# Two small weight transfers made twice as wide, and kept in the first ring slot

## The chip, the cores and the metric

The kernel runs on one core of one Trainium2 chip. The metric is the device time of one execution in microseconds; lower is better. Profiles show one execution on the chip. TensorE is PE in them (its weight loads are PEld), VectorE is DVE, ScalarE is ACT, GpSimd is POOL and SyncE is SP, which issues all transfers here.

## The reference

A block for decoding: a layer norm, attention of one new token against a cache, and an MLP, with a residual after each. Batch 4, model width 448, 16 query heads over 8 groups of cached keys and values, head width 256, and the last 1024 positions of the cache.

```python
W = min(4096, max(256, Sk // 4))                    # 1024
q = (x @ wq).reshape(B, Sq, Hq, Dh)...              # [4, 16, 1, 256]
k, v = the last W rows of k_cache and v_cache, each shared by two heads
p = softmax(einsum("bhqd,bhkd->bhqk", q, k) * Dh ** -0.5)
A(x) = einsum("bhqk,bhkd->bhqd", p, v).reshape(B, Sq, Hq * Dh) @ wo
B(x) = gelu(layernorm(x) @ w1 + b1) @ w2 + b2
h = x + A(layernorm(x))
out = h + B(layernorm(h))
```

All is float32. The keys, values and weights that must be read are 88 MB.

## The kernel before, in words

The work goes group by group over the eight groups of keys and values. For a group, `project_q` multiplies the normed input by the group's 448 x 512 query weights and turns the result; `scores` multiplies the query by the keys in two halves of 512 positions; `softmax` and `transpose_p` follow; `values` multiplies by the values; `finish` turns the output and adds its product with the output weights to `acc`. After the last group come the second layer norm and the MLP, with `w1` and `w2`.

The width of 448 is three blocks of 128 rows and one of 64. In the packed weights of a group the last 64 rows lie as 128 rows of 256 columns: the upper half of the partitions holds the second 256 columns. `wq_parts` lists the matmuls of a projection: three with 128 rows and 512 columns, and then either two with 128 rows and 256 columns (each with an input `yT` that is zero in the half that doesn't belong), or, if `last` is given, one with 64 rows and 512 columns.

All data come through a ring of three slots of 128 partitions x 15872 elements (`ring`, filled by `load` at L58), in one queue of transfers on SP, in the order written. The slot `t0` takes the first query weights with the input (`wq0`), and the keys of group 0 with three blocks of the query weights of group 1 (`k0`). The other slots are refilled in turn: `ta` from `la`, `tb` from `lb`, `tc` from `lc`, `td` from `ld`, twice over, and then three slots `te` for the last keys and values and the MLP's weights. The tc load takes the place of `t0`, td that of ta, and so on. Each load waits on SP until the old content of its slot has been read.

The last 64 rows of the query weights of group 1 do not go with `k0`. They come in two transfers of 32 rows of 2048 bytes (L265) into a tile of their own, `wq1_last`; each takes its source from 8 rows of 5 pieces in HBM, of which 4 are read and the fifth is padding. They stand in the queue between `k0` and the first `la`.

The instructions of PE, SP and ACT stand in the order of the code; each engine works through its own, and waits on semaphores.

Of the kernel before, what the change touches and what calls it, by code (L numbers as in the profile page):

```python
# [8 lines left out]
F32 = mybir.dt.float32  # L9
# [6 lines left out]
B, D = 4, 448  # L16
HQ, HKV, SK, DH = 16, 8, 4096, 256
# [3 lines left out]
P = 128  # L21
H = P // 2
# [4 lines left out]
Q = 32  # L27
CACHE = NKC * B * DH
HALF = CACHE // 2
WEIGHTS = 4 * D  # L30
SLOT = CACHE + 2 * WEIGHTS + HALF
COLUMNS = ND * B + 4 + 4 * 4
EPS = 1e-5
SCALE = DH ** -0.5

@with_exitstack
def block_kernel(ctx: ExitStack, tc, wq0, k0, wq1, la, lb, lc, ld, k7, vo, w1, w2, out):
    nc = tc.nc
    const = ctx.enter_context(tc.tile_pool(name="const", bufs=1))
    ring = ctx.enter_context(tc.tile_pool(name="ring", bufs=3))  # L40
    work = ctx.enter_context(tc.tile_pool(name="work", bufs=2))
# [9 lines left out]
    def slot(name):  # L51
        return ring.tile([P, SLOT], F32, tag="r", name=name)

    def load(t, at, src, pieces=None):
        dst = t[:, at : at + src.shape[-1]]
        at = 0
        for n in pieces or (src.shape[-1],):
            nc.sync.dma_start(dst[:, at : at + n], src[:, at : at + n])  # L58
            at += n
        return dst  # L60

    def cut(t, sizes):
        parts, at = [], 0
        for n in sizes:
            parts.append(t[:, at : at + n])
            at += n
        return parts


    def wq_parts(t, last=None):  # L70
        parts = [(a, yT[:, a, :], slice(0, 512), t[:, a * 512 : (a + 1) * 512]) for a in range(3)]
        if last is not None:
            return parts + [(3, yT[:H, 3, :], slice(0, 512), last)]
        for i in range(2):
            parts.append((3, yT[:, 3 + i, :], slice(i * 2 * P, (i + 1) * 2 * P), t[:, 3 * 512 :]))
        return parts


    def keys(t):
        return t.rearrange("p (c b k) -> p c b k", c=2, b=B)  # L80

    def chunks(t):
        v = t.rearrange("p (c b d) -> p c b d", b=B, d=DH)
        return [v[:, c : c + 2] for c in range(0, v.shape[1], 2)]
# [17 lines left out]

    yT = const.tile([P, ND + 1, Q], F32, name="yT")
    nc.vector.memset(yT, 0.0)
    wq1_last = const.tile([H, 512], F32, name="wq1_last")
    zT = const.tile([P, ND, Q], F32, name="zT")
    nc.vector.memset(zT, 0.0)

# [34 lines left out]
    def rsqrt(dst, var, name):  # L143
        ve = work.tile(list(dst.shape), F32, tag="ve", name=f"ve_{name}")
        nc.vector.tensor_scalar_add(ve, var, EPS)
        nc.gpsimd.tensor_tensor(dst, ve, mhalf[: dst.shape[0], : dst.shape[1]], op=ALU.pow)


    def project_q(g, parts):
        pq = ps_m.tile([P, 512], F32, tag="m", name=f"pq{g}")  # L150
        for j, y, cols, w in parts:
            nc.tensor.matmul(pq[j * Q : (j + 1) * Q, cols], y, w, start=True, stop=True)  # L152
        qs = work.tile([P, 512], F32, tag="qs", name=f"qs{g}")
        nc.scalar.copy(qs, pq)  # L154

        pt = ps_m.tile([P, 2 * REP, P], F32, tag="m", name=f"pqt{g}")
        for i in range(2 * REP):
            nc.tensor.transpose(pt[:, i, :], qs[:, i * P : (i + 1) * P], ident)  # L158
        sm = work.tile([P, 2 * REP, B], F32, tag="sm", name=f"sm{g}")
        nc.vector.tensor_reduce(  # L160
            sm, pt.rearrange("p i (j q) -> p i q j", j=4)[:, :, :B, :], axis=AX.X, op=ALU.add
        )

        src = sm.rearrange("p (r c) b -> p c b r", r=REP)
        for i in range(2):
            nc.vector.tensor_copy(qT[g % 2][:, :, :, i * REP : (i + 1) * REP], src)
# [13 lines left out]
    def softmax(g, parts):  # L180
        halves, mx = zip(*parts)
        nm = work.tile([P, 1], F32, tag="nm", name=f"nm{g}")
        nc.vector.tensor_max(nm, mx[0], mx[1])
        nc.vector.tensor_scalar_mul(nm, nm, -SCALE)  # L184
        p = once.tile([P, 2 * 512], F32, tag="p", name=f"p{g}")
        sums = work.tile([P, 2], F32, tag="sums", name=f"sums{g}")
        for h in range(2):
            nc.scalar.activation(  # L188
                p[:, h * 512 : (h + 1) * 512], halves[h], AF.Exp, bias=nm, scale=SCALE,
                accum_out=sums[:, h : h + 1],  # L190
            )
        rec = work.tile([P, 1], F32, tag=f"rec{g % 3}", name=f"rec{g}")
        nc.vector.tensor_add(rec, sums[:, 0:1], sums[:, 1:2])
        nc.vector.reciprocal(rec, rec)
        return p, rec

    def scores(g, kt):
        return [scores_half(g, h, kt[h]) for h in range(2)]

    def transpose_p(g, p):  # L200
        for h in range(2):
            pt = ps_t.tile([P, 4, P], F32, tag="t", name=f"ppt{g}_{h}")
            for c in range(4):
                nc.tensor.transpose(pt[:, c, :], p[:, (4 * h + c) * P : (4 * h + c + 1) * P], ident)  # L204

            src = pt.rearrange("p (c i) (b q) -> p c i b q", i=2, b=B)
            for i in range(2):
                nc.vector.tensor_copy(  # L208
                    pT[g % 2][:, 2 * h : 2 * h + 2, :, i * REP : (i + 1) * REP], src[:, :, i, :, :REP]
                )  # L210


    def values(g, vt, po, pairs=range(NKC // 2)):
        for c in pairs:
            for b in range(B):
                nc.tensor.matmul(  # L216
                    po[b * Q : (b + 1) * Q], pT[g % 2][:, c, b, :], vt[c][:, :, b, :],
                    start=(c == 0), stop=(c == NKC // 2 - 1),
                )
# [35 lines left out]
    def po_tile(g, pool=ps_o, tag="o"):  # L255
        return pool.tile([P, 2, DH], F32, tag=tag, name=f"po{g}")


    t = slot("t0")
    wqt, xT, b2T, b1T = cut(load(t, 0, wq0), (WEIGHTS, ND * B, 4, 4 * 4))  # L260
    wqt = wq_parts(wqt)
    xT = xT.rearrange("p (a b) -> p a b", a=ND)
    ka, kb, wqt1 = cut(load(t, WEIGHTS + COLUMNS, k0), (HALF, HALF, 3 * 512))
    for i in range(2):
        nc.sync.dma_start(  # L265
            wq1_last[i * Q : (i + 1) * Q, :], wq1[i].rearrange("e (p c) -> e p c", c=512)[:, :4, :]
        )
    d = work.tile([P, ND, B], F32, tag="d", name="d_x")
    centred(d, xT, "x")
# [21 lines left out]
        nc.scalar.copy(rs[:, at : at + cols], pr.rearrange("p i c -> p (i c)")[:, :cols])  # L291

    parts = scores(0, [keys(ka), keys(kb)])
    project_q(1, wq_parts(wqt1, wq1_last))
    p, rec = softmax(0, parts)
    transpose_p(0, p)

    def finish(g, po, rec, wt):
        transposed_output(g, po, rec)
        add_output(g, output_weights(wt))  # L300

    for g in (0, 3):
        ka, kb, wqt, va = cut(load(slot(f"ta{g}"), 0, la[g // 3]), (HALF, HALF, WEIGHTS, HALF))
        parts = scores(g + 1, [keys(ka), keys(kb)])
        project_q(g + 2, wq_parts(wqt))
        p, rec_next = softmax(g + 1, parts)
        transpose_p(g + 1, p)
        po = po_tile(g)
        va = chunks(va)
        values(g, va, po, range(0, 2))  # L310

        vb, wot, ka, kb = cut(load(slot(f"tb{g}"), 0, lb[g // 3]), (HALF, WEIGHTS, HALF, HALF))
        values(g, va + chunks(vb), po, range(2, 4))
        p, rec_then = softmax(g + 2, scores(g + 2, [keys(ka), keys(kb)]))
# [29 lines left out]
    p, rec_last = softmax(g + 1, scores(g + 1, kt))  # L344
# [212 lines left out]
```

## Time and profile before

| | |
|---|---|
| time, median of 3 runs | 213.93 us (213.82 to 213.99) |
| profiled execution: time | 214.16 us |
| its span, first to last instruction | 212.4 us |
| granted TensorE clock, mean | 0.854 |
| PE busy | 133.9 us (63%) |
| DVE busy | 39.0 us (18%) |
| ACT busy | 22.1 us (10%) |
| data moved | 88.43 MB, mean 416 GB/s |
| packets of the load queue | 3248, 88.30 MB, 96.9% of 16 DMA engines' span |

The span is counted from the first to the last instruction of the core; the time has some 1.8 us more around it. A load is one transfer that is cut into packets, here one per row of the destination, which 16 DMA engines move side by side. It has landed when its last packet has. In a row such as `206.00 1.71 PE L469 ... [0.69 <-DMA te<-w]` the first number is the start, the second the length, and the bracket says how long the engine was idle before and for what.

### The profile page before, as it was taken

The numbers are of one execution on the slowest core, as the hardware profiler recorded it, in microseconds if no ns is written. First come the engines' busy times: TensorE is split into PE (matmuls) and PEld (weight loads), VectorE is DVE, ScalarE is ACT, GpSimd is POOL, SyncE is SP. The second block draws the span as 40 slices with busy tenths as digits, with TensorE's granted clock in tenths as the row PEclk, the third lists the DMA queues.
The fourth block names the chain that finished last, engine by engine and source line by source line (L and its number), as shares of the span: only waits on it lengthen the run. The fifth ranks groups of instructions, "written<-read, shape, count | busy, mean of one in ns | idle before, by whom it ended". The sixth has DMA issues, their size and how long they took to land.

```text
span 212.4 us, 2302 instructions
## 1 busy us (share of the span) xinstructions
PE 133.9 (63%) x976; PEld 48.3 (23%) x976; DVE 39.0 (18%) x170; ACT 22.1 (10%) x54; POOL 5.0 (2%) x16
## 2 busy tenths in 40 slices
PE   0469805843950696288398098138708879978984
PEld 0342201310220221022123023013202323224432
DVE  1520300410230003022013013100301223112310
ACT  2011300300020100030003002001000302010311
POOL 5100000000000000000000000000000000000200
PEclk9999995995896559589969759856985999999999
DMA  7999898999999999999999999999989999999991
GB/s 294 425 396 534 361 488 361 491 394 475 407 395 529 395 407 430 451 403 459 424 424 488 403 395 505 395 430 419 478 350 460 430 429 394 440 400 444 419 384 52
DMA packets 3257, 88.43 MB, mean 416 GB/s; under 512 B 368, under 2 KB 624, under 8 KB 1328
## 3 DMA queue, kind: packets, MB, share of 16 engines
q1 hardware_dynamic: 3248, 88.30, 96.9%
q8 instruction: 7, 0.11, 0.2%
q14 instruction: 2, 0.02, 0.0%
HBM read 88.23 MB, written 0.07 MB: 416 GB/s over the span
## 4 chain that ended last, share of the span: by engine, by line
DMA 78%; PE 16%; SPq 2%; DVE 1%; issue 1%; ACT 1%; ACTq 0%
DMA tb<-lb 22%; DMA ta<-la 21%; DMA td<-ld 20%; DMA te<-w 14%; PE s L172 6%; PE po L216 4%; SPq L58 2%; PE ppt L204 1%; PE pq L152 1%; PE acc L245 1%; PE pa L469 1%; PE py L479 1%; SPq L265 1%; PE pqt L158 1%; ACT qs L154 1%
## 5 line engine op out<-in xcount | busy, mean ns | idle before, releaser
L177 DVE TENSOR_REDUCE mx<-s 128x1 f32<-128x512 f32 x16 | 11.1, 691 | 57.8 <-PE s L172 57.8
L172 PE MATMUL s<-ta,qT 128*32 128x512 f32 x64 | 10.7, 831 | 10.3 <-DMA ta<-la 10.3
L154 ACT COPY qs<-pq 128x512 f32<-128x512 f32 x8 | 4.7, 585 | 113.3 <-PE pq L152 113.3
L188 ACT ACTIVATE p<-s,nm 128x512 f32<-128x512 f32 x16 | 10.9, 687 | 46.1 <-DVE nm L184 46.1
L233 DVE TENSOR_SCALAR o<-po,rec 128x512 f32<-128x512 f32 x8 | 6.0, 750 | 48.5 <-PE po L216 48.5
L216 PE MATMUL po<-tb,pT 128*32 128x512 f32 x32 | 7.2, 1051 | 12.2 <-DMA tb<-lb 12.2
L172 PE MATMUL s<-td,qT 128*32 128x512 f32 x32 | 7.1, 1042 | 12.1 <-DMA td<-ld 12.1
L152 PE MATMUL pq<-tc,yT 128*32 128x512 f32 (+1 forms) x20 | 3.9, 891 | 16.6 <-DMA tc<-lc 16.6
L204 PE MATMUL ppt<-ident,p 128*128 128x128 f32 x64 | 10.5, 287 | 0.7 <-ACT p L188 0.4
L216 PE MATMUL po<-tc,pT 128*32 128x512 f32 x64 | 10.4, 813 | 0.0
L158 PE MATMUL pqt<-ident,qs 128*128 128x128 f32 x32 | 6.6, 341 | 6.0 <-ACT qs L154 6.0
L204 PEld LDWEIGHTS ppt<-ident,p 128*128 128x128 f32 x64 | 6.7, 141 | 6.3 <-ACT p L188 6.3
L160 DVE TENSOR_REDUCE sm<-pqt 128x16 f32<-128x64 f32 x8 | 1.8, 224 | 34.4 <-PE pqt L158 34.4
L216 PE MATMUL po<-te,pT 128*32 128x512 f32 x64 | 7.5, 595 | 0.5 <-DMA te<-vo 0.5
L172 PE MATMUL s<-tb,qT 128*32 128x512 f32 x64 | 7.4, 607 | 0.0
L216 PE MATMUL po<-td,pT 128*32 128x512 f32 x64 | 7.3, 595 | 0.0
L237 PE MATMUL pot<-ident,o 128*128 128x128 f32 x32 | 5.2, 286 | 2.7 <-DVE o L233 2.7
L158 PEld LDWEIGHTS pqt<-ident,qs 128*128 128x128 f32 x32 | 4.2, 169 | 11.4 <-ACT qs L154 9.7
L351 PE MATMUL warm<-idle 128*32 128x512 bf16 x22 | 6.8, 382 | 0.0
L172 PEld LDWEIGHTS s<-ta,qT 128*32 128x32 f32 x64 | 2.6, 148 | 17.7 <-issue 13.7
L208 DVE COPY pT<-ppt 128x16 f32<-128x16 f32 x32 | 4.7, 171 | 7.6 <-PE ppt L204 7.6
L172 PE MATMUL s<-t,qT 128*32 128x512 f32 x32 | 5.4, 833 | 0.5 <-DMA t<-k 0.5
(134 smaller groups left out, 112.4 us busy)
## 6 DMA issues: line engine op xcount, KB each, us to landing
tc<-lc SPq DMA_DIRECT2D x2, 7936.0 KB, 47.0
td<-ld SPq DMA_DIRECT2D x2, 7936.0 KB, 44.0
ta<-la SPq DMA_DIRECT2D x2, 7040.0 KB, 38.1
tb<-lb SPq DMA_DIRECT2D x2, 7040.0 KB, 43.2
te<-vo SPq DMA_DIRECT2D x1, 4992.0 KB, 28.1
t<-k SPq DMA_DIRECT2D x1, 4864.0 KB, 15.8
te<-k SPq DMA_DIRECT2D x1, 4096.0 KB, 37.8
te<-vo SPq DMA_DIRECT2D x1, 3072.0 KB, 14.8
```

Of the source, the lines that this page charges most:

```text
L152: nc.tensor.matmul(pq[j * Q : (j + 1) * Q, cols], y, w, start=True, stop=True)
L154: nc.scalar.copy(qs, pq)
L158: nc.tensor.transpose(pt[:, i, :], qs[:, i * P : (i + 1) * P], ident)
L172: nc.tensor.matmul(s[b * Q : (b + 1) * Q, :], qT[g % 2][:, c, b, :], kt[:, c, b, :], start=(c == 0), stop=(c == 1),)
L177: nc.vector.reduce_max(m, s, axis=AX.X)
L188: nc.scalar.activation(p[:, h * 512 : (h + 1) * 512], halves[h], AF.Exp, bias=nm, scale=SCALE, accum_out=sums[:, h : h + 1],)
L204: nc.tensor.transpose(pt[:, c, :], p[:, (4 * h + c) * P : (4 * h + c + 1) * P], ident)
L208: nc.vector.tensor_copy(pT[g % 2][:, 2 * h : 2 * h + 2, :, i * REP : (i + 1) * REP], src[:, :, i, :, :REP])
L216: nc.tensor.matmul(po[b * Q : (b + 1) * Q], pT[g % 2][:, c, b, :], vt[c][:, :, b, :], start=(c == 0), stop=(c == NKC // 2 - 1),)
L233: nc.vector.tensor_scalar_mul(o, po, rec)
L237: nc.tensor.transpose(pt[:, i, c], o[:, i, c * P : (c + 1) * P], ident)
L351: nc.tensor.matmul(warm[:Q], idle[:, :Q], idle, start=True, stop=True)
```

## The change

The last 64 rows of the query weights of group 2 go the same way as those of group 1. Both stand side by side in `wq_rest`, 64 rows of 1024 columns, which come in the same two transfers, now of 32 rows of 4096 bytes. They are no longer put into a tile of their own but into the slot `t0`, behind the keys of group 0 (`REST`). The first `la` load (`la0`) loses these rows: its query weights are 1536 columns wide instead of 1792. The second (`la1`) stays as it was. The projection of group 2 takes its last block from `rest`, with one matmul instead of two.

```diff
+REST = WEIGHTS + COLUMNS + CACHE + 3 * 512
...
-    wq1_last = const.tile([H, 512], F32, name="wq1_last")
...
     ka, kb, wqt1 = cut(load(t, WEIGHTS + COLUMNS, k0), (HALF, HALF, 3 * 512))
+    rest = t[:H, REST : REST + 2 * 512]
     for i in range(2):
         nc.sync.dma_start(
-            wq1_last[i * Q : (i + 1) * Q, :], wq1[i].rearrange("e (p c) -> e p c", c=512)[:, :4, :]
+            rest[i * Q : (i + 1) * Q], wq_rest[i].rearrange("e (p c) -> e p c", c=2 * 512)[:, :4, :]
         )
...
-    project_q(1, wq_parts(wqt1, wq1_last))
+    project_q(1, wq_parts(wqt1, rest[:, :512]))
...
     for g in (0, 3):
-        ka, kb, wqt, va = cut(load(slot(f"ta{g}"), 0, la[g // 3]), (HALF, HALF, WEIGHTS, HALF))
+        n = WEIGHTS if g else 3 * 512
+        ka, kb, wqt, va = cut(load(slot(f"ta{g}"), 0, la[g // 3]), (HALF, HALF, n, HALF))
         parts = scores(g + 1, [keys(ka), keys(kb)])
-        project_q(g + 2, wq_parts(wqt))
+        project_q(g + 2, wq_parts(wqt, None if g else rest[:, 512:]))
...
-    la = np.concatenate([k[1:5:3], wq[2:6:3], va[0:4:3]], axis=2)
+    la0 = np.concatenate([k[1], wq[2][:, : 3 * 512], va[0]], axis=1)
+    la1 = np.concatenate([k[4], wq[5], va[3]], axis=1)
...
-    wq1 = np.asarray(A_wq).reshape(D, HKV, 512)[3 * P :, 1].reshape(2, 8, 4 * 512)
-    wq1 = np.concatenate([wq1, np.zeros((2, 8, 512), np.float32)], axis=2)
+    wq_rest = np.asarray(A_wq).reshape(D, HKV, 512)[3 * P :, 1:3].reshape(2, 8, 8 * 512)
+    wq_rest = np.concatenate([wq_rest, np.zeros((2, 8, 1024), np.float32)], axis=2)
```

On SP, at the start of the queue, the loads stand as follows before (destination, source, partitions x elements; DMAHW0 to DMAHW7 are the semaphores that transfers raise, PE and DVE those of the engines):

```order
L58 DMA t_129<-wq 128x1828
L58 DMA t_129<-k 128x9728
L265 DMA wq_last<-wq 32x1x512 x2
L58 DMA ta_247<-la 128x14080
L58 DMA tb_321<-lb 128x14080
L58 DMA tc_390<-lc 128x15872 [waits DMAHW0_49,DMAHW1_49,DVE_49,PE_49]
L58 DMA td_450<-ld 128x15872 [waits DMAHW4_49,PE_49]
```

And now:

```order
L60 DMA t_128<-wq 128x1828
L60 DMA t_128<-k 128x9728
L267 DMA t_128<-wq_rest 32x1x1024 x2
L60 DMA ta_246<-la 128x13824
L60 DMA tb_319<-lb 128x14080
L60 DMA tc_388<-lc 128x15872 [waits DMAHW1_49,DMAHW2_49,DMAHW0_49,DMAHW3_49,DVE_49,PE_49]
L60 DMA td_448<-ld 128x15872 [waits DMAHW4_49,PE_49]
```

The order is the same. The two small transfers write into the slot of `wq0` and `k0`, with rows of 1024 elements instead of 512; the la rows have 256 elements less; and the tc load, which takes that slot, waits for the two small transfers as well.

On PE, from the scores of group 1 to the end of the projection of group 2, before:

```order
L172 MATMUL s_0_249<-ta_247,qT_112 32x512 [waits DVE_49,DMAHW4_49,PE_49,Pool_49]
L172 MATMUL s_0_249<-ta_247,qT_112 32x512 x7
L172 MATMUL s_1_260<-ta_247,qT_112 32x512 [waits PE_49]
L172 MATMUL s_1_260<-ta_247,qT_112 32x512 x7
L152 MATMUL pq_271<-ta_247,yT 32x512 [waits PE_49]
L152 MATMUL pq_271<-ta_247,yT 32x512 x2
L152 MATMUL pq_271<-ta_247,yT 32x256 x2
```

And now:

```order
L173 MATMUL s_0_248<-ta_246,qT_111 32x512 [waits DVE_49,DMAHW4_49,PE_49,Pool_49]
L173 MATMUL s_0_248<-ta_246,qT_111 32x512 x7
L173 MATMUL s_1_259<-ta_246,qT_111 32x512 [waits PE_49]
L173 MATMUL s_1_259<-ta_246,qT_111 32x512 x7
L153 MATMUL pq_270<-ta_246,yT 32x512 [waits PE_49]
L153 MATMUL pq_270<-ta_246,yT 32x512 x2
L153 MATMUL pq_270<-t_128,yT 32x512
```

The last two matmuls became one, which reads the first slot; since it comes after the scores of the la load, `t0` is read until then.

More of the change, by code (lines that the diff above doesn't have):

```diff
@@ L36, in block_kernel @@
 @with_exitstack
-def block_kernel(ctx: ExitStack, tc, wq0, k0, wq1, la, lb, lc, ld, k7, vo, w1, w2, out):
+def block_kernel(ctx: ExitStack, tc, wq0, k0, wq_rest, la0, la1, lb, lc, ld, k7, vo, w1, w2, out):
     nc = tc.nc
+    la = (la0, la1)
     const = ctx.enter_context(tc.tile_pool(name="const", bufs=1))
@@ L541 @@
     arrays = {
-        "wq0": np.concatenate([wq[0], xT, b2, b1], axis=1), "k0": k0, "wq1": wq1, "la": la, "lb": lb, "lc": lc, "ld": ld, "k7": k[7], "vo": vo, "w1": w1, "w2": w2,
+        "wq0": np.concatenate([wq[0], xT, b2, b1], axis=1), "k0": k0, "wq_rest": wq_rest, "la0": la0, "la1": la1, "lb": lb, "lc": lc, "ld": ld, "k7": k[7], "vo": vo, "w1": w1, "w2": w2,
     }
```

## The prediction, on record before the changed kernel ran

> **What bounds the kernel now.** I read the page first (its DMA row, the queues, the chain that ended last), then the timeline of the last microseconds, then the stages of the tail, and last the packet records behind the DMA row.
>
> ```profile
> span 212.4 us, 2302 instructions
> ...
> DMA  7999898999999999999999999999989999999991
> ...
> q1 hardware_dynamic: 3248, 88.30, 96.9%
> q8 instruction: 7, 0.11, 0.2%
> q14 instruction: 2, 0.02, 0.0%
> ...
> DMA 78%; PE 16%; SPq 2%; DVE 1%; issue 1%; ACT 1%; ACTq 0%
> ```
>
> The loads keep 16 DMA engines busy for 96.9% of the span; between the first slice and the last the digit is 8 or 9 everywhere. So the time is the bytes that the busiest DMA engine must move, plus a tail. A second thing stands in the queue rows: seven fetches of 16 KB and two of 8 KB of instructions share those engines.
>
> Who waits at the end is in the timeline (start, length, then in brackets the idle time before the piece and its releaser):
>
> ```profile
> 205.34 0.33 ACT L462 COPY gT<-put 64x8 f32<-64x8 f32 x2 [1.19 <-DVE gT L459]
> 206.00 1.71 PE L469 MATMUL pa<-te,gT 128*32 128x448 f32 x16 [0.69 <-DMA te<-w]
> 207.56 0.56 PEld L479 LDWEIGHTS py<-te,gT 128*32 128x32 f32 x24 [0.67 <-DMA te<-w]
> 209.20 0.11 PEld L479 LDWEIGHTS py<-te,gT 128*4 128x4 f32 x8 [0.23 <-DMA te<-w]
> 209.67 0.29 DVE L485 TENSOR_TENSOR res<-py,hb 128x128 f32<-128x128 f32 x1 [4.42 <-PE py L479]
> ```
>
> PE waits for w2 three times, and for its very last piece (`w2t[13]`) at 209.20. The compute chain has its operand gT at 205.34 + 0.33 = 205.67, so it is 0.33 us ahead of the 206.00 at which the data lets PE start. DMA decides the end, but by 0.33 us only.
>
> A load is landed when the slowest of its engines is done. The stages of the tail show that they are not done together (the last two columns are the busy share of the 16 engines and GB/s):
>
> ```profile
> 206.50:207.00 0.50, 0.50 (x12) 0.14 (x6) 0.00 (x0) 0.00 (x0) 0.00 (x0) 1.00 0.89 351
> 207.00:207.50 0.50, 0.50 (x8) 0.00 (x0) 0.00 (x0) 0.00 (x0) 0.00 (x0) 1.00 0.55 215
> 207.50:208.00 0.50, 0.50 (x22) 0.44 (x21) 0.00 (x0) 0.17 (x1) 0.00 (x0) 1.00 0.47 179
> 208.00:208.50 0.50, 0.50 (x20) 0.21 (x15) 0.00 (x0) 0.36 (x1) 0.00 (x0) 1.00 0.11 39
> 208.50:209.00 0.50, 0.50 (x24) 0.39 (x24) 0.00 (x0) 0.00 (x0) 0.00 (x0) 1.00 0.02 7
> ```
>
> From 207 on the share falls 0.55, 0.47, 0.11, 0.02: half of the engines are idle while one works on to the end. Which half is the question of this case.
>
> **Which engines carry the small transfers.** The trace does not name the DMA engine of a packet, but each engine's packets follow one another within some 30 ns, so that 16 chains can be followed from the packet records. This table is worked out from them (end of an engine's part of a load, us; "low" are the eight chains that hold 2048-byte packets):
>
> ```
> first la load, low  : 33.26 33.35 33.38 33.41 33.44 33.51 33.52 33.52
> first la load, high : 32.61 32.70 33.08 33.14 33.15 33.15 33.25 33.27
> first w2 load, all  : 202.80 203.41 203.48 203.56 203.64 203.71 203.75 204.26
>                       204.37 204.52 204.71 204.75 204.79 204.79 204.90 205.36
> first packet 1.72; second load (lb): first chain done 49.24, another 49.73
> third load (lc): first chain done 67.99, that other 69.91; small transfers landed 17.35
> increments of the semaphores of the two 32-row transfers: 9 and 9; of every other load: 16
> 16 KB fetches begin at 38.92 63.78 99.82 127.52 164.07 185.87 202.65; 8 KB fetches at 45.80 201.97
> median packet: 2048 B 84 ns, 3584 B 140, 5376 B 206, 56320 B 2080, 63488 B 2345
> ```
>
> The two small transfers run on eight engines only, four rows each. [...]
>
> A 16 KB fetch holds one engine up by about 1.45 us: the chain that ended at 49.73 in the second load ends at 69.91 in the third, 20.18 later, where the first chain takes 18.75. Of the first six fetches five fell on chains of the high half, and one on a chain that cannot be told from a low one at the same offset; both 8 KB fetches fell on low ones (0.7 to 0.9 us each). The seventh, at 202.65, fell on a chain that would have ended its part of the first w2 load at 203.73. The undisturbed chains up there are the low ones (203.56 to 203.75); the high ones that were never held up stand at 202.80 to 203.48. So the engine that ends last, at 205.36, is a low one: 203.73 + 1.63.
>
> **The change, part by part.**
>
> *Bytes.* 128 KB leave the first la load, whose rows shrink from 56320 to 55296 bytes on all 16 engines, and come back as 2048 more bytes in each of the 64 small rows, on the eight low engines. The time of a 4096-byte packet is not in the trace: between 140 (3584) and 206 (5376) it is 140 + 66 x 512/1792 = 159 ns. Bounds are two 2048-byte packets, 168 ns, and the rate of the large ones, 4096 x 2080/56320 = 151 ns; I take 159. Low engines gain 8 x (159 - 84) = 0.60 us (0.54 to 0.67). The 1024 bytes off a large row are worth 1024 x (2345 - 2080)/7168 = 37.9 ns, over 8 rows 0.30 us for every engine. Sum: low engines end 0.30 us later (0.24 to 0.37), high ones 0.30 us earlier. Bytes in all, and transfers in number, stay.
>
> *Where that ends up.* The last engine is low, so all w2 pieces land 0.30 us later, PE starts at 206.30 instead of 206.00, and the waits at 207.56 and 209.20 move with it: +0.30 us.
>
> *One matmul less in the projection of group 2.* The two 256-column matmuls with 128 rows become one with 64 rows and 512 columns.
>
> ```profile
> L152 PE MATMUL pq<-ta,yT 128*32 128x512 f32 x12 | 2.1, 592 | 0.0
> L152 PE MATMUL pq<-ta,yT 128*32 128x256 f32 x8 | 2.1, 379 | 0.0
> ...
> 34.13 5.40 PE L172 MATMUL s<-ta,qT 128*32 128x512 f32 x32 [7.12 <-DMA ta<-la]
> 39.34 1.05 PE L152 MATMUL pq<-ta,yT 128*32 128x512 f32 x10
> 43.10 1.92 PE L216 MATMUL po<-ta,pT 128*32 128x512 f32 x16
> ...
> PE po L216 <- DMA tb<-lb: 12.2, 2, 6.4
> ```
>
> Each fp32 matmul has two records, so ten become eight: about 2 x 379 - 592 = 0.17 us of overlapped records saved at most. PE then waits up to 6.4 us for tb, so this is worth nothing; tb is what is late next. The cover would have to shrink by 6 us before it counts.
>
> *The first slot is held longer.* The third group of weights now lies in slot `t0`, which the tc load reuses. The issue of tc waited for the second projection (PE at 23.28); now it waits for the projection after the la load.
>
> ```profile
> 1.62 1.55 SPq L265 DMA_DIRECT2D wq_last<-wq  x2
> ...
> 23.40 0.33 SPq L58 DMA_DIRECT2D tc<-lc  x1
> 45.08 0.33 SPq L58 DMA_DIRECT2D td<-ld  x1
> 60.57 0.33 SPq L58 DMA_DIRECT2D ta<-la  x1
> ```
>
> 39.34 + 1.05 + 0.30 is 40.7, so tc goes out near 41, about 17 us later. What hides it: the tb load in front keeps every engine busy until the first is done with it at 49.24. From an issue to its first packet is 1.0 us (0.73, first packet 1.72), so some 7 us are left. Behind tc on SP stands td, which waits for PE's reads of the first la slot (43.10) and went out at 45.08; tc at 41 does not delay it. Cost nothing; from an issue after 48 on, each microsecond would be lost one for one on all engines.
>
> *The second projection* waits for the small transfers, which now end 0.60 us later.
>
> ```profile
> 23.28 1.04 PE L152 MATMUL pq<-wq_last,yT 64*32 64x512 f32 x2
> ```
>
> They were landed at 17.35 and would be at 17.95, five microseconds ahead: nothing. The SP issues of the two stay two of 0.75 us, before the queue fills. The scores of the la load start 0.30 us later (34.13) and PE waits for tb all the same.
>
> *Sum.* 0.30 + 0 + 0 + 0. The profiled execution took 214.16 us, 1.76 around its span; it would take 214.46. It stands 0.23 above the median of 213.93, so the median to expect is 213.93 + 0.30 = 214.2, or +0.14%. A measurement of this kernel tells about 0.2% (0.43 us) from no change, so by that bound this is a small loss that counts as no change.
>
> **The rivals.**
>
> *The seventh fetch falls on a high engine (faster).* The engine of a fetch is not set by the kernel's text. Then the last one ends at about 203.48 - 0.30 + 1.63 = 204.81, like the low one with an 8 KB fetch (204.52 + 0.30 = 204.82): 0.54 before 205.36. The compute chain is only 0.33 us ahead, so the gain ends there: 213.6 at best, perhaps 0.1 lower if the earlier waits for v ease too.
>
> ```profile
> 188.94 2.78 PE L216 MATMUL po<-te,pT 128*32 128x512 f32 x24 [0.20 <-DMA te<-vo]
> ```
>
> That wait of 0.20 us is the last before the compute chain to gT. Against it: three runs of before within 0.17 us speak for a fixed place, and nothing in the change moves fetches but PE's four records less. Chance 0.18, 0.11 of it beyond 0.2%.
>
> *A fetch meets an engine that an earlier one has already held up (slower).* The price is what the seventh costs on top of a low engine with an 8 KB fetch: 204.52 + 0.30 + 1.63 = 206.45, 1.1 us above 205.36, or 215.0. It decides once such a chain is the target. Before, the seventh met an unheld chain; the same doubt as above. Chance 0.11.
>
> *The queue runs dry before tc (slower).* If the release of `t0` is seen later than I think, past 48, all engines stand. At an issue of 50 it is some 2 us: 216. Speaks for it: it would be the load with the least lead of all that follow the start. Against: 7 us of margin. Chance 0.05.
>
> *The small transfers spread evenly (no change).* The increments above exclude it as the trace stands, so that it would need the new rows to be split otherwise: each engine then gains and loses the same bytes, 213.9. Chance 0.04. [...]
>
> **How the numbers follow.** The forecast, low engines last by 0.30 more, has 0.62; its own range is 214.0 to 214.6, from 0.24 to 0.37 and a fetch whose price has differed by 0.18 (1.45 and 1.63), with the 0.17 that three runs differ. What of it lies above 0.43 us, 0.20, counts as slower. Slower: 0.20 + 0.11 + 0.05 = 0.36. Faster: 0.11. Same: 0.42 + 0.07 + 0.04 = 0.53. The range goes from 213.6 (the fast rival) to 214.9, short of most of the two slow rivals.
>
> **What would show it.** Right: in the packet records low chains end the first la load about 0.6 us further behind the high ones than now; the packet of 4096 bytes takes 151 to 168 ns; PE's last wait for w2 ends near 209.5; tc is issued near 41 and the DMA share around 49 has no hole; PE's wait for tb stays near 6 us. Wrong: the last engine of the first w2 load is a high one or one with two fetches, the tc issue stands after 48, or the 32-row transfers' semaphores take 16 increments.

## The result, and the profile after

The changed kernel took 214.19 us (median of 20 executions, 213.96 to 215.60), against 213.88 (20 executions, 213.68 to 214.07) for the kernel before on the same chip. The ratio is 1.0023, with a 95% interval from 1.0012 to 1.0034: a little slower. Seventeen of the 20 executions lie between 213.96 and 214.29; three, the profiled one among them, took 215.49 to 215.60, and are taken up below. The two parts can be kept apart: by the medians the change costs 0.31 us (0.14%), and the three executions add about 3 x 1.35/20 = 0.20 us to the mean.

The page of the changed kernel, in the rows that answer to those shown of before; the row PEclk is the granted clock of TensorE in 40 slices:

```profile
span 213.7 us, 2299 instructions
...
PEclk9999965895796589579669759856985999999979
DMA  7989999999999999999999999999989998999970
...
q1 hardware_dynamic: 3248, 88.30, 96.3%
...
DMA 77%; PE 17%; SPq 2%; DVE 1%; issue 1%; ACT 1%; ACTq 0%
```

The same packets and bytes, three instructions less in all (four less on PE), and a span 1.3 us longer than 212.4. The last DMA digit is 0, where it was 1: the last piece of w2 landed at 209.14, against 209.16 before, and the span goes on for longer behind it. The timeline of the tail, as read of before:

```profile
205.17 0.33 ACT L465 COPY gT<-put 64x8 f32<-64x8 f32 x2 [1.19 <-DVE gT L462]
205.99 3.21 PE L472 MATMUL pa<-te,gT 128*32 128x448 f32 x16 [0.85 <-DMA te<-w]
208.93 1.10 PE L482 MATMUL py<-te,gT 128*32 128x128 f32 x24
...
211.05 0.29 DVE L488 TENSOR_TENSOR res<-py,hb 128x128 f32<-128x128 f32 x1 [5.97 <-PE py L482]
```

`pa`, the first product that needs w2, starts at 205.99, as it did before (206.00). The 16 matmuls of it then take 3.21 us instead of 1.71, and the rest follows late. The products behind it, from 208.93, carry no bracket: PE does not wait for w2 there any more. The stages say why; here is 206.0 to 209.5 of the kernel before and then of the changed one (length, busy time of PE, PEld, DVE, ACT and POOL with records, then granted clock, DMA share, GB/s):

```profile
206.00:209.50 3.50, 3.50 (x72) 1.58 (x72) 0.00 (x0) 0.53 (x1) 0.00 (x0) 1.00 0.42 165
```

```profile
206.00:209.50 3.50, 3.50 (x29) 1.38 (x33) 0.00 (x0) 0.18 (x1) 0.00 (x0) 0.51 0.40 158
```

PE is busy throughout in both, with 72 records before and 29 now, at clock 1.00 and 0.51. So the profiled execution of the changed kernel shows two things that must be told apart: where the data lands, and the clock at which the last products run.

**One number keeps them apart.** From the start of `pa` to the end of the whole execution, the time is nearly the same in all profiled executions whose last stage had the full clock, whatever the kernel: 214.16 - 206.00 = 8.16 (before), and in the experiments below 213.76 - 205.60 = 8.16, 214.31 - 206.15 = 8.16, 215.63 - 207.48 = 8.15, 214.07 - 205.81 = 8.26, 214.72 - 206.47 = 8.25, 215.83 - 207.76 = 8.07. With half the clock it is 215.53 - 205.99 = 9.54 (changed kernel), and 9.49, 9.46 and 9.47 in experiments. So an execution with the full clock and a `pa` at 205.99 would have taken 214.15, which is where the seventeen lie (median 214.18); half the clock costs some 1.35 us on top, which is where the three lie. And backwards: the median of before, 213.88, belongs to a `pa` near 205.72. The profiled execution of before, with its `pa` at 206.00, was itself late by 0.28 us. Against an ordinary execution of before the start of `pa` moved by about +0.27 us.

The first part of the kernel, where the forecast had costed the other edits at nothing: the changed kernel's timeline of PE and of SP's queue.

```profile
34.32 5.82 PE L173 MATMUL s<-ta,qT 128*32 128x512 f32 x32 [8.50 <-DMA ta<-la]
39.96 1.04 PE L153 MATMUL pq<-ta,yT 128*32 128x512 f32 x6
40.93 1.04 PE L153 MATMUL pq<-t,yT 64*32 64x512 f32 x2
...
42.00 0.33 SPq L60 DMA_DIRECT2D tc<-lc  x1
46.63 0.33 SPq L60 DMA_DIRECT2D td<-ld  x1
```

And its waits (total, times, longest):

```profile
PE po L217 <- DMA tb<-lb: 10.3, 2, 5.2
```

The projection reads its 64 rows from the first slot `t` in two records; the tc load is issued at 42.00 (23.40 before); PE still waits 5.2 us for tb. And its stages around 49, where the first engine is free for tc:

```profile
45.00:49.00 4.00, 1.56 (x16) 0.26 (x8) 0.01 (x1) 0.00 (x0) 0.00 (x0) 1.00 1.01 438
49.00:51.00 2.00, 0.00 (x0) 0.00 (x0) 0.00 (x0) 0.00 (x0) 0.00 (x0) 0.50 1.10 473
```

The DMA share (the column before the last) shows no hole.

### The profile page after: what moved, and what is told of

Read it like the earlier page. It is cut to its first block, busy times and chain, and to the rows that moved or that the text cites. A ratio compares the mean times of both kernels' runs of the same rounds, so it can differ in the third digit from the quotient of the medians.

```text
span 213.7 us, 2299 instructions
## 1 busy us (share of the span) xinstructions
PE 137.5 (64%) x974; PEld 49.0 (23%) x974; DVE 39.0 (18%) x170; ACT 22.1 (10%) x54; POOL 5.0 (2%) x16
## 4 chain that ended last, share of the span: by engine, by line
DMA 77%; PE 17%; SPq 2%; DVE 1%; issue 1%; ACT 1%; ACTq 0%
DMA tb<-lb 22%; DMA ta<-la 21%; DMA td<-ld 20%; DMA te<-w 14%; PE s L173 6%; PE po L217 4%; SPq L60 2%; PE pa L472 2%; PE pq L153 1%; PE ppt L205 1%; PE acc L246 1%; PE py L482 1%; SPq L267 1%; PE pqt L159 1%; ACT qs L155 1%
## 5 line engine op out<-in xcount | busy, mean ns | idle before, releaser
L173 PE MATMUL s<-ta,qT 128*32 128x512 f32 x64 | 11.8, 902 | 11.0 <-DMA ta<-la 11.0
L217 PE MATMUL po<-tc,pT 128*32 128x512 f32 x64 | 9.9, 772 | 0.0
L173 PE MATMUL s<-tb,qT 128*32 128x512 f32 x64 | 8.5, 672 | 0.0
L153 PE MATMUL pq<-t,yT 128*32 128x512 f32 (+2 forms) x20 | 5.0, 742 | 2.9 <-DVE yT L277 2.9
```

Of the source, the lines that this page charges most:

```text
L173: nc.tensor.matmul(s[b * Q : (b + 1) * Q, :], qT[g % 2][:, c, b, :], kt[:, c, b, :], start=(c == 0), stop=(c == 1),)
L217: nc.tensor.matmul(po[b * Q : (b + 1) * Q], pT[g % 2][:, c, b, :], vt[c][:, :, b, :], start=(c == 0), stop=(c == NKC // 2 - 1),)
```

## The experiments

The theories: (A) the forecast's, that the eight low engines got 0.30 us more to move and one of them ends last; (B) that the longer hold of the first slot delays tc; (C) that the order of the work or the code's own fetches moved; (D) that the time comes from the clock of the last stage.

### The change once more

The changed kernel, unaltered, once more for its profile and its time.

> The changed kernel once more, for a profile of an ordinary execution. Low engines last (the low eight DMA engines carry the wider rows, and one of them ends last): about 0.3 us over the kernel before, packets of 4096 bytes of 151 to 168 ns, low chains about 0.3 us later at the end of the first w2 load. Slot held longer (the late issue of the tc load costs the time): the same 0.3 us, but with a hole in the DMA share near 49 to 51 us. Clock (all of it is PE at half clock in the last microseconds, as in the profile of the changed kernel at 215.53): most runs level with before, some 1.3 us above.

214.25 us (12 executions, 213.97 to 215.54), ratio 1.0020 [1.0009, 1.0030]. Its profiled execution is the single one of the 12 above 214.4, and again has half the clock in the last stage. Its timeline, and behind it the stage:

```profile
206.05 3.16 PE L472 MATMUL pa<-te,gT 128*32 128x448 f32 x16 [0.72 <-DMA te<-w]
```

```profile
206.00:209.50 3.50, 3.45 (x28) 1.49 (x32) 0.00 (x0) 0.18 (x1) 0.00 (x0) 0.52 0.41 161
```

Before that stage its packet records can be followed engine by engine, as in the prediction (worked out from the records, ends in us):

```
first la load, low  : 33.43 to 33.81, mean 33.64     high: 32.29 to 33.03, mean 32.75
first w2 load, low  : 203.73 204.49 205.43 203.78 204.03 204.90 203.65 204.43
first w2 load, high : 202.42 204.07 204.56 204.53 204.42 204.00 204.66 203.02
median packet       : 2048 B 84 ns (before); 4096 B 159 ns (all 64 of the changed kernel)
```

After the first la load the low engines are 0.90 us behind the high ones; before it was 0.38, in the execution of the slot experiment below 0.30: 0.52 to 0.60 more, the forecast's 0.60. The packet of 4096 bytes takes 159 ns. The last engine of the first w2 load, at 205.43, is a low one. Theory A's links stand one by one. The other eleven executions have a median of 214.25, so that the clock (theory D) adds to single executions and does not make the 0.3 us.

### The longer hold of the slot alone

The kernel before, with an extra matmul (its product is overwritten) that reads the first slot in the projection of group 2, so that `t0` is held nearly as long as in the change:

```
+    wq1_last = t[:H, WEIGHTS + COLUMNS + CACHE + 3 * 512 :][:, :512]
...
-        project_q(g + 2, wq_parts(wqt))
+        again = [] if g else [(0, yT[:H, 3, :], slice(0, 512), wq1_last)]
+        project_q(g + 2, again + wq_parts(wqt))
```

> The kernel before, with the last rows of group 1 (still 2048 bytes each) in the first slot, and one matmul more at the start of the projection of group 2 that reads them, so that the slot is held as long as in the change; its product is overwritten. No byte moves to another engine. Low engines last: level with before within 0.1 us, tc issued near 41. Slot held longer: 0.3 us above before. Clock: most runs level, some 1.3 us above.

213.89 us (11 executions), ratio 1.0000 [0.9991, 1.0008]. From its timeline:

```profile
40.67 0.33 SPq L58 DMA_DIRECT2D tc<-lc  x1
...
205.60 1.71 PE L470 MATMUL pa<-te,gT 128*32 128x448 f32 x16 [0.39 <-DMA te<-w]
208.81 0.11 PEld L480 LDWEIGHTS py<-te,gT 128*4 128x4 f32 x8 [0.24 <-DMA te<-w]
```

tc is issued at 40.67 instead of 23.40 (42.00 in the changed kernel), and the time stays. Theory B falls. This execution also shows what the profiled one of before did not: an ordinary end of the old distribution, `pa` at 205.60.

### Twice the bytes in the same places

The change, with small rows of 8192 bytes, of which the second half is zeros that nobody reads:

```
-    rest = t[:H, REST : REST + 2 * 512]
+    rest = t[:H, REST : REST + 4 * 512]
...
-            rest[i * Q : (i + 1) * Q], wq_rest[i].rearrange("e (p c) -> e p c", c=2 * 512)[:, :4, :]
+            rest[i * Q : (i + 1) * Q], wq_rest[i].rearrange("e (p c) -> e p c", c=4 * 512)[:, :4, :]
...
```

> The change with rows of 8192 bytes in the two small transfers; the second half of each is zeros that nothing reads. Low engines last: a packet of 8192 bytes takes about 311 ns, so low engines end 8 x (311 - 159) = 1.2 us later than in the change, and the time is 1.2 us above the change, 1.5 above before. Slot held longer: like the change, 0.3 above before, or little more. Spread over all engines: 256 KB more on 16 engines, 0.6 us above the change.

215.56 us (6 executions), ratio 1.0084 [1.0067, 1.0102]: 1.31 us above the change with rows of 4096 bytes (214.25). One of the six, the profiled one at 216.83, has half the clock in the last stage:

```profile
207.37 3.12 PE L472 MATMUL pa<-te,gT 128*32 128x448 f32 x16 [0.95 <-DMA te<-w]
```

The packet takes 309 ns, 8 x (309 - 159) = 1.20 us more for each low engine. With 1.8 us between the groups no chain can be taken for one of the other group (worked out from the packet records, ends in us):

```
first la load, low  : 34.70 to 34.97     high: 32.33 to 32.92
first w2 load, low  : 205.04 205.19 205.14 206.73 205.11 205.96 204.87 205.63
first w2 load, high : 202.49 204.07 204.43 204.61 204.45 203.07 204.40 204.51
```

All eight low engines end after all eight high ones, and the last one, 206.73, is the low engine that had the seventh 16 KB fetch. Of the high ones six were held up by a fetch, and two (202.49 and 203.07) not. What is added to the low engines is paid in full at the end: 1.31 us there, where 256 KB shared by all 16 engines would have been some 0.6 (an estimate, at the mean of 416 GB/s). Theory A holds.

### The same rows from 16 engines

If the change costs time because eight engines carry it, sixteen should carry it for less. The source as 16 rows of two pieces instead of 8 of four, the same bytes and destination:

```
-            rest[i * Q : (i + 1) * Q], wq_rest[i].rearrange("e (p c) -> e p c", c=2 * 512)[:, :4, :]
+            rest[i * Q : (i + 1) * Q], wq_rest[i].rearrange("e (p c) -> e p c", c=2 * 512)[:, :2, :]
...
-    wq_rest = np.asarray(A_wq).reshape(D, HKV, 512)[3 * P :, 1:3].reshape(2, 8, 8 * 512)
+    wq_rest = np.asarray(A_wq).reshape(D, HKV, 512)[3 * P :, 1:3].reshape(2, 16, 4 * 512)
...
```

> The change with the source of the two small transfers laid out as 16 rows of 2 pieces, so that 16 engines share them. Low engines last: low engines move 8 rows of 4096 bytes less one half, 0.64 us less than in the change, high ones 0.64 us more; against before low ones are 0.34 us earlier and high ones 0.33 us later; the last engine of the first w2 load then ends near 205.0 to 205.2 instead of 205.36, and the time is 0.1 to 0.3 us below before, 0.4 to 0.6 below the change. Slot held longer: no better than the change, about 0.3 us above before. Clock: like the change.

215.43 us (5 executions, 215.23 to 215.63), ratio 1.0069 [1.0056, 1.0082]: a miss, and a large one. First the two stages at the start in the changed kernel, then in this one (last columns: DMA share, GB/s), then the start of `pa` in this one's timeline:

```profile
16.00:18.00 2.00, 1.63 (x12) 0.64 (x14) 0.02 (x1) 0.84 (x2) 0.00 (x0) 1.00 1.34 569
18.00:34.00 16.00, 7.11 (x52) 2.50 (x44) 2.87 (x13) 1.93 (x5) 0.00 (x0) 0.83 1.02 443
```

```profile
16.00:18.00 2.00, 0.99 (x8) 0.59 (x10) 0.03 (x1) 0.85 (x2) 0.00 (x0) 1.00 1.83 482
18.00:34.00 16.00, 9.81 (x52) 3.00 (x44) 2.87 (x13) 1.94 (x5) 0.00 (x0) 0.98 0.93 397
```

```profile
207.48 1.71 PE L472 MATMUL pa<-te,gT 128*32 128x448 f32 x16 [0.21 <-DMA te<-w]
```

From 16 to 18, while the small rows are moved, the engines' packets take more time (share 1.83 instead of 1.34) and move less (482 GB/s instead of 569); behind them, from 18 to 34, it is 397 instead of 443. In the packet records the 4096-byte packet takes 301 ns in the median (458 at most) instead of 159, and packets of the first la load up to 3611 ns, where the median is 2041. Summed over the engines and divided by 16, the small packets cost 1.07 us instead of 0.64 and those of the la load 17.41 instead of 16.33: 0.43 + 1.08, 1.5 us of each engine's time. So the split over 16 engines did take place (the semaphore of each small transfer has 16 increments, where it has 9 in the kernel before and in the changed one); but the slower packets cost more than the unevenness had.

### One transfer of 64 rows

The same 64 rows in a single transfer, from a source of 16 rows of four pieces:

```
-    for i in range(2):
-        nc.sync.dma_start(
-            rest[i * Q : (i + 1) * Q], wq_rest[i].rearrange("e (p c) -> e p c", c=2 * 512)[:, :4, :]
-        )
+    nc.sync.dma_start(rest, wq_rest.rearrange("e (p c) -> e p c", c=2 * 512)[:, :4, :])
...
```

> The change with one transfer of 64 rows of 4096 bytes in place of two of 32, its source 16 rows of 4 pieces, so that 16 engines take 4 rows each. If the loss of the version with 16 engines (1.55 us above before) came from engines that write into the same 32 partitions side by side, packets of 4096 bytes and the first la packets stay near 159 and 2041 ns here, or are slowed less, and the time is 0.2 us below before to 0.8 above. If 16 engines as such, or a source of 16 rows, cost it: 215.4 again.

214.74 us (5 executions, 214.63 to 214.99), ratio 1.0044 [1.0030, 1.0057]. The same stages, and the start of `pa` in the timeline:

```profile
16.00:18.00 2.00, 1.32 (x8) 0.57 (x10) 0.01 (x1) 0.83 (x2) 0.00 (x0) 1.00 1.64 571
18.00:34.00 16.00, 8.30 (x52) 2.74 (x44) 2.86 (x13) 1.94 (x5) 0.00 (x0) 0.89 1.00 433
```

```profile
206.47 1.71 PE L469 MATMUL pa<-te,gT 128*32 128x448 f32 x16 [0.21 <-DMA te<-w]
```

Half as bad, and just over the range that was expected if engines in the same 32 partitions were the cause (up to 0.8 us above before; it is 0.84): 571 and 433 GB/s, small packets 159 ns in the median and 324 at most, la packets up to 2716; 0.11 us for the small ones and 0.51 for the la load over the changed kernel. Both forms lose at one place: in the small packets, and in the la packets behind. That the rows of this one went to 16 engines, as expected, no figure here shows.

### No small transfers at all

The kernel before, with all of the second group's weights in the load of k0: every engine gets the same bytes, nothing in 32 rows is left.

```
-    ka, kb, wqt1 = cut(load(t, WEIGHTS + COLUMNS, k0), (HALF, HALF, 3 * 512))
-    for i in range(2):
-        nc.sync.dma_start(
-            wq1_last[i * Q : (i + 1) * Q, :], wq1[i].rearrange("e (p c) -> e p c", c=512)[:, :4, :]
-        )
+    ka, kb, wqt1 = cut(load(t, WEIGHTS + COLUMNS, k0), (HALF, HALF, WEIGHTS))
...
```

> The kernel before without the two small transfers: the last 64 rows of the query weights of group 1 go with the first keys, as 256 columns of 128 rows, and the projection of group 1 has two matmuls more of 256 columns in place of one of 512. Every engine moves the same number of bytes. Low engines last: low engines end 0.67 - 0.30 = 0.37 us earlier than before, high ones 0.30 later; the last one of the first w2 load is then 0.15 to 0.35 us earlier than before, and the time 0.1 to 0.3 us shorter. If the low half is not the one that ends last: 0.3 us longer.

214.09 us (11 executions, 214.05 to 214.42), ratio 1.0013 [1.0004, 1.0021]: a miss, 0.19 us slower than before, where a gain was expected. Its tail:

```profile
205.63 0.33 ACT L457 COPY gT<-put 64x8 f32<-64x8 f32 x2 [1.19 <-DVE gT L454]
205.81 1.71 PE L464 MATMUL pa<-te,gT 128*32 128x448 f32 x16 [0.20 <-DMA te<-w]
208.97 0.11 PEld L474 LDWEIGHTS py<-te,gT 128*4 128x4 f32 x8 [0.19 <-DMA te<-w]
```

The last landings of the first w2 load by its semaphore are 205.50, 205.50, 205.51 and 205.67: several engines at once, where the changed kernel has one straggler (204.96, 205.19, 205.85). That is what an even share does when the fetches are not even: the engines held up by fetches, most of them high, now carry as much as the others. In the packet records the four that end the first w2 load last, at 205.04, 205.04, 205.06 and 205.16, had each been held up by one of the first six 16 KB fetches; in the kernel before four such high engines ended at 204.71 to 204.79, and 0.30 more is what the even share gives them. There they carry less than the low ones, which covers part of the fetches.

It gives the scale of the two forms laid out for 16 engines too: against this even share they lose 215.43 - 214.09 = 1.34 and 214.74 - 214.09 = 0.65 us, where their packets cost 1.5 and 0.62 us more.

### Less idle time on PE, and more

Three kernels for the clock. First the change without the PE work at one place that is there to keep PE busy (`fill(2)` after the softmax of the last group):

```
-    fill(2)
     transpose_p(g + 1, p)
```

> The change without the two matmuls at about 177 us that only keep PE busy; their result is not used. Is the half clock in the last microseconds of the change's profiled execution (206.0 to 209.4) set by how busy PE has been since 165? Then it comes later or not at all, and the profiled execution takes 214.2 us like the others. If it is set by a grid of time alone, it stays and the profiled execution takes 215.5. Where the waits for transfers stand does not change: w2 lands within 0.2 us of the change.

214.31 us (11 executions, 213.96 to 214.77), ratio 1.0023 [1.0014, 1.0031]. Its profiled execution, at 214.31, is one of the ordinary ones, and it shows the change's end at full clock; the timeline, and behind it three stages:

```profile
205.62 0.33 ACT L464 COPY gT<-put 64x8 f32<-64x8 f32 x2 [1.19 <-DVE gT L461]
206.15 1.71 PE L471 MATMUL pa<-te,gT 128*32 128x448 f32 x16 [0.55 <-DMA te<-w]
209.33 0.11 PEld L481 LDWEIGHTS py<-te,gT 128*4 128x4 f32 x8 [0.21 <-DMA te<-w]
```

```profile
176.00:179.80 3.80, 1.70 (x14) 0.62 (x7) 1.18 (x6) 1.45 (x4) 0.00 (x0) 1.00 0.94 404
179.80:183.20 3.40, 3.26 (x14) 0.93 (x16) 0.52 (x5) 0.00 (x0) 0.00 (x0) 0.50 1.00 426
206.00:209.40 3.40, 3.25 (x68) 1.58 (x72) 0.00 (x0) 0.53 (x1) 0.00 (x0) 1.00 0.42 163
```

`pa` at 206.15, the last wait for w2 at 209.33, the last stage at 1.00, and 214.31 in all: the same time as the change within its spread. Where PE lost its fill it was busy 1.70 of 3.8 us (3.63 in the changed kernel), and the next 3.4 us have half the clock. In the granted clock such stretches are 3.41 us long: 206.03 to 209.44 in the changed kernel, 206.16 to 209.58 in its repetition, 207.53 to 210.94 with rows of 8192, 179.83 to 183.24 here. Elsewhere half and full clock last longer, but in the profiles of before and of the changed kernel always a whole multiple of that (6.83, 10.24, 13.65, 40.96 and 47.79 us). That an idle stretch brings the half clock behind it is the author's reading of this order (1.70 us of PE from 176.00 to 179.80, then clock 0.50; 3.63 us in the changed kernel, then 1.00); no run shows a rule for it. The run does not tell whether the fill had a part in the last stage: none of its 11 executions has the 1.35 us on top, but of the change's 32 only four have.

In the last stage the idle stretch is the wait for w2 in front of `pa`. It is 0.85, 0.72 and 0.95 us in the three executions with half the clock, and 0.69 (before), 0.55, 0.39, 0.21, 0.21 and 0.20 in those with the full clock. A wait that the change makes some 0.3 us longer comes to the side where the clock falls. This fits these nine executions, and it fits that it befell 4 of the changed kernel's 32 executions (two of them profiled, two by their time) against none of the 75 of the kernel before; that the wait is the cause was not shown by a run that lengthens it alone. That 0.69 and 0.72 fall on different sides goes, by the author's estimate, with the place at which the clock can change, counted in steps of 3.41 us from its last change before (164.02 in the profile of before, 165.07 in that of the changed kernel). In the three executions with half the clock it changed just behind the start of `pa` (206.03, 206.16 and 207.53), so that the 3.41 us before it hold all of the wait, and PE was busy for 2.17 to 2.40 us of them. In the profile of before, so counted, the place lies at 204.97, in front of the wait, and the 3.41 us from there have 2.72 us of PE; in the other five with the full clock it is 2.58 or more. This does not settle it either: in the changed kernel the 3.41 us from 151.41 have only 1.89 us of PE, in the tail of the change without the matmuls (below) 3.41 us have 2.28, and the clock stays full behind both.

Then both kernels without any of the matmuls that only keep PE busy:

```
-    fill(2)
     transpose_p(g + 1, p)
-    keep_warm(2, warm0)
...
-    keep_warm(1, warm)
...
```

> The change without all matmuls that only keep PE busy (22 in bf16 and two in fp32, 52 records); their results are not used. Seventh fetch on a low engine sets the end: with 52 records less PE reaches the place of the seventh fetch later, after the first w2 load, whose last chain then ends some 0.8 us earlier (near 204.7 instead of 205.4 to 205.5) and in a cluster with others; the time falls by up to 0.3 us, where the compute chain takes over, unless PE is slower for want of them. If the fetch has no part in it, w2 lands at 205.9 as in the change.

> The kernel before without the same matmuls; their results are not used. Seventh fetch sets the end: w2 lands with no straggler, and this one and the change without them differ by less than the 0.3 us of the kernels with them, since high engines with a fetch then end last, and those move less in the change. If the wider rows as such cost 0.3 us, the same 0.3 us stand between the two. The time of both is that of the compute chain if PE is slower without them.

216.98 us (6 executions, 215.83 to 217.92) and 216.37 (6, 216.07 to 217.84): ratios 1.0144 [1.0116, 1.0172] and 1.0129 [1.0107, 1.0151] to the kernel before. By their times they cannot tell the change's 0.3 us, with a spread of 2 us. By their transfers they answer what was expected of them, and theory C with it. Without that work on PE the seventh 16 KB fetch begins at 203.96 and 203.25, when its engine is through with the first w2 load (worked out from the packet records, us):

```
                               seventh fetch   last two ends of the first w2 load   w2 landed
changed kernel                 202.71          204.68, 205.34                       205.85
kernel before                  202.65          204.90, 205.35                       205.87
before, slot held longer       202.87          204.83, 204.95                       205.47
change, without the matmuls    203.96          204.54, 204.72                       205.28
before, without the matmuls    203.25          204.85, 204.89                       205.46
```

With the fetch out of the way there is no straggler, the load ends at 204.72 where near 204.7 was expected, and w2 lands 0.18 us earlier with the change than without it, not 0.3 later (one execution each). So the wider rows cost their 0.3 us because the seventh fetch falls on one of the engines that carry them; and in the kernels with the matmuls that fetch begins at nearly the same time with the change and without it, so that C does not explain the loss. In the changed one, a stage and then the timeline of the tail:

```profile
200.20:203.60 3.40, 3.40 (x21) 0.57 (x24) 0.75 (x4) 0.89 (x1) 1.08 (x2) 0.50 1.00 420
```

```profile
207.45 0.21 DVE L450 COPY gT<-put 128x48 f32<-128x48 f32 x1 [1.29 <-PE put L448]
207.75 0.33 ACT L453 COPY gT<-put 64x8 f32<-64x8 f32 x2 [1.19 <-DVE gT L450]
207.76 1.71 PE L459 MATMUL pa<-te,gT 128*32 128x448 f32 x16 [0.35 <-issue]
```

Half the clock falls into the compute chain, which is then the bound: `pa` starts at 207.76, though w2 was there at 205.28. One thing in it corrects the prediction: `pa` starts 0.10 us after the DVE copy of gT ends (207.66), while the ACT copy is still running (207.75 to 208.08). By the kernel's text all of `pa` needs only the DVE part: it reads blocks 0 to 7 of gT, and the DVE copies blocks 0 to 11. In the other one half the clock fell into the last stage as well, from 208.47 on, after 3.41 us with 1.91 us of PE.

## Why the prediction was right, and where not

**The sum and its term: right.** +0.30 us was forecast, +0.31 measured by the medians (0.37 in the repetition). The links were measured one by one: 159 ns for the packet of 4096 bytes, where the estimate between 140 and 206 had given 159; 55296 bytes in 2041 ns, 39 less than 56320, for 37.9 forecast; low engines 0.52 to 0.60 further behind; a low engine last. In the mean of four executions with the change (the changed kernel, its repetition, without the fill, without the matmuls) and three without (before, slot held longer, without the matmuls), the low engines end the first la load at 33.60 against 33.34, 0.26 later, and the high ones at 32.71 against 33.04, 0.33 earlier; 0.30 was forecast for each. That the sum agrees to 0.01 us is closer than its parts do, and in part luck. Rows twice as long cost 1.31 more for 1.20 us of packets. The ratio of 1.0023 lies a little over the 0.2% that the prediction named as the bound of a difference, and its interval on both sides of it; 0.31 us alone is 0.14%, as forecast, and the rest is the three long executions.

**Each step costed at nothing: right.** The slot held to 40.67 costs 0.00 (interval -0.09% to +0.08%). The cover of the shorter projection, the wait for tb, is still 5.2 us, where some 6 were forecast. The small transfers landed at 17.84, for 17.95 forecast. tc went out at 42.00, a microsecond later than "near 41", and in the slot experiment at 40.67; no hole at 49.

**"Only 0.33 us ahead": wrong.** The prediction took the ACT copy of gT, done at 205.67, for what `pa` needs. It needs the DVE copy, which the profile of before shows like this:

```profile
205.04 0.21 DVE L459 COPY gT<-put 128x48 f32<-128x48 f32 x1 [1.29 <-PE put L457]
```

It was done at 205.25, and the compute chain was some 0.75 us ahead. The limit put on the fast rival, a gain of 0.33 us at most, was too tight. In the runs with an early `pa` the wait for w2 still stands in front of it: 0.39 at 205.60.

**The profiled execution of before: mis-sized.** The sum was made on an execution of 214.16 us and put onto the median by subtracting 0.23. That is sound for a constant shift. But the place where the extra 0.23 lay was in the tail itself: a single straggler, landed at 205.87 where 205.24 and 205.37 were the next, and 205.47 in the slot experiment. So "PE's last wait near 209.5" stood 0.2 too high (209.33), the start of `pa` at 206.30 as well (205.99 to 206.15), and the distance between the last low engine and the others looked larger than it usually is. This led to the gain that two experiments expected of an even share (the one with 16 engines lost more by its slower packets): with the low engines some 0.3 us less ahead of the rest, moving bytes from them to the held-up high ones makes those last.

**The fast rival, a fetch on another engine: not seen with the change.** In the repetition and in the run without the fill the last engine is a low one as well, and with rows of 8192 the seventh 16 KB fetch is on a low engine beyond doubt. In these three and the changed kernel's first profile the first six 16 KB fetches are on six different high engines and the seventh on a low one. In the executions without the change the groups lie too close for this to be told; there the end of the load differs by 0.40 us (205.35 and 204.95) with where the engine of that fetch stands. The other rivals did not come about: no low engine with two fetches was the last (205.43 and 205.50, not 206.45), the queue did not run dry, and the transfers stayed on eight engines (in the changed kernel too each one's semaphore has 9 increments: one early, at 2.83 and 3.60, and eight when its rows land, from 16.99 to 17.20 and from 17.62 to 17.84).

**Not foreseen: the clock of the last stage.** The prediction spoke of a wait that grows by 0.3 us and of nothing that follows from a longer wait on PE. In 4 of 32 executions a half clock followed, for 3.41 us where a profile shows it, at 1.35 us each. The profile of before shows the full clock behind its wait of 0.69 us, so that no row of it priced this step.

**What stays open.** What makes the forms laid out for 16 engines slow. Both are slower than the one on eight engines (medians and highest of the small packets: eight engines 159 and 159 ns, 64 rows in one transfer 159 and 324, twice 32 rows 301 and 458); why, and why the last is the slowest, no run shows, since the trace does not name the engine of a packet. Nor is it shown what sets the engine of a code fetch.

## What to carry to other kernels

When the DMA engines bound a kernel, its end is that of the single latest engine (205.34 us for the first w2 load in the changed kernel, with the next at 204.68): count the bytes of each engine, with the code fetches that hold one up, and not their sum; an even share was not the best one where the fetches fell unevenly (214.09 us against 213.90). Before a small effect is priced in a tail, look at where the profiled execution stands among the others, and take the stragglers of its tail from more than one execution. A wait on PE shortly before the last products may cost more than its length, by way of the clock that follows: 1.35 us on top in 4 of 32 executions here, though no run lengthened the wait alone.

## What the runs showed of the hardware

- The time of a packet is close to a line through zero: 84 ns for 2048 bytes, 159 for 4096, 309 for 8192, 2041 for 55296. That is 42, 40, 39 and 38 ns per 1024 bytes, so that rows of 4096 bytes cost hardly more than long ones.
- Spreading a small transfer over more engines made it slower: rows of 4096 bytes, in transfers of 32, took 301 ns each in the median on 16 engines and 159 on eight, and the large packets behind them were slowed too, up to 3611 ns for 2041.
- The engines that fell behind stayed behind. With rows of 8192 bytes the low engines are some 2.2 us behind the high ones at 33 us; at 205 the low ones without a fetch (204.87 to 205.19) are 1.8 to 2.7 behind the high ones without one (202.49 and 203.07).
- One 16 KB fetch of instructions held the engine that it fell on up by 1.43 us (20.18 us for a load where another engine took 18.75). The first w2 load ended at 205.34 in the changed kernel, where the seventh fetch came before the end of its engine's part, and at 204.72 without the matmuls, where it came behind.
- Stretches of half and of full clock on TensorE lasted whole multiples of 3.41 us (3.41, 6.83, 10.24, 13.65). In the tails of nine executions a half clock came after 3.41 us in which PE was busy for 2.17 to 2.40 us, and not after 2.58 or more; elsewhere 1.89 and 2.28 us were enough to keep the full clock.
